# A planned scan-and-gate kernel: VectorE's steps in the head put into a fixed order, the fourth tile copied out by VectorE

## The chip, the cores and the metric

The kernel runs on one core of a Trainium2 chip. The metric is device time in microseconds (us). Before the change it is 181.62 us, the median of seven runs that lie between 181.51 and 181.90.

## The reference, cut to what matters

The input x is 2048 tokens by 512 channels. It is normalised per token, and two branches use the result. Branch A is a diagonal state space model: a complex projection, a recurrence over all 2048 tokens, a complex projection back and a skip. Branch B is a gated feed-forward net of width 1376. The output joins both.

```python
xn = layernorm(x)                       # per token, over 512 channels
Lam_bar = exp(dt * Lam)                 # dt = exp(log_dt), 512 complex numbers
Bu = einsum("bld,pd->blp", xn, ((Lam_bar - 1) / Lam)[:, None] * (B_re + 1j * B_im))
h[t] = Lam_bar * h[t-1] + Bu[t]         # t = 0 .. 2047
s = 2 * einsum("blp,dp->bld", h, C_re + 1j * C_im).real + xn * Dskip
g = silu((gelu(xn @ w_gate) * (xn @ w_up)) @ w_down)
out = x + s * g
```

All data are bf16.

## The kernel before, in words

**Tiling.** The tokens go in four stages of 512 (s = 0 to 3), each of four tiles of 128 tokens (m = 0 to 3). The matmuls need the normalised tile with the channels on the partitions, so each tile is turned. In stage 0, the head, TensorE turns it by four 128x128 transposes into half a PSUM bank (`transposed`, L415 to L425, called by `head_t`, L695), and ScalarE copies the result into `xnT` (L423). In the later stages a transposing DMA does it (`dma_t`).

**The head.** The first x tiles, the log step sizes, the gate weights `wg` and `wu` in three column chunks, the second stage's x, the projection BT and more weights are loaded one after the other; the SP queue issues them in a written chain (`dma_first`, L307, L331 to L343). For each tile, VectorE takes the statistics of 512 channels (L396), joins them (L399), adds a small constant to the variance (L405), POOL raises that to the power -0.5 (L402, tile `rs`), and VectorE normalises (L437, tile `xn`). In between VectorE also prepares the tables of cosines and sines: it copies the imaginary parts out of PSUM (L371), multiplies by the step size (L372), and does four steps on 196 angles (L656, L658, L659, L660), after which ScalarE takes two sines (L661, L662). POOL and ScalarE narrow these to bf16 (L664, L665), and VectorE builds the tables by six products and sums of 2048 columns (L676).

The first column chunk of gate and up matmuls of stage 0 (`gate_pair`, 384 columns, L470) runs tile by tile behind the transposes. It goes to three PSUM slots of two banks in turn; the fourth tile uses the two banks `ybank`, which the transposes use as well. The next chunk (512 columns) starts again with slot 0. ScalarE empties these banks by a copy (L475) and by the gelu (L476), which needs another function table than the sines; `early` orders the first gelu behind the sines. VectorE multiplies the two (L477).

`damping` (L687) turns four more small vectors by one tiny matmul (L690) through `ybank[0]`; its result, `rho`, is raised by POOL (L402) and needed by the scans.

**The body.** `half` (L592) projects with BT (L602), rotates by the tables (L616, L624 or L628), scans along time (L635) and rotates back. `gate_tile` and `down_pair` (L491, L534) are branch B; `y_tile` (L543) multiplies the states by C2 into `ybank` (L564), and VectorE joins the branches (L568 to L576). In the later stages ScalarE seeds `ybank` with the skip (L560). The output leaves by DMA on SP, one tile of 128 tokens at a time.

**What sets the order.** Each step is handed to a planner (`Plan`, L24) with its engine, an estimated cost, the time its result takes to reach others (`lag`), the names it reads and writes, and perhaps a rank. TensorE's steps are chained in the order in which the program adds them. The other engines' orders come from list scheduling by the longest remaining path plus rank, in six rounds forward and backward, and then from 3000 random trials on the start times, with a fixed seed, of which the best by the planner's own estimate is kept. The steps are then emitted by planned start. `after` adds an order without data; `_lag` (L59) says how long one step's end must lie before another's start. `urgent` (L391) gives the first two tiles' statistics and norms higher ranks.

Of the kernel before, what the change touches and what calls it, by code (L numbers as in the profile page):

```python
# [13 lines left out]
ALU = mybir.AluOpType  # L14
# [9 lines left out]
class Plan:  # L24

    def __init__(self):
        self.steps = []
        self.wrote = {}  # L30
        self.read = {}
        self.last_pe = None

    def add(self, eng, cost, emit, reads=(), writes=(), lag=0.05, table=None, not_before=0.0, rank=0.0, after=()):
# [161 lines left out]
def kernel(  # L196
# [17 lines left out]
    nc = tc.nc  # L214
    P = 128
# [174 lines left out]

    def urgent(s, m):  # L391
        return (60.0, 30.0, 0.0, 0.0)[m] if s == 0 else 0.0

    def stats(s, m):
        def f():
            V.bn_stats(out=st[:, s, m, :], in_=x_tok[:, s * M + m, :])  # L396
        rank = urgent(s, m)
        dve(512, f, [("x", s, m)], [("st", s, m)], base=0.12, rank=rank)
        dve(6, lambda: V.bn_aggr(out=mv[:, s, m, :], in_=st[:, s, m, :]), [("st", s, m)], [("mv", s, m)], base=0.08, rank=rank)  # L399

# [3 lines left out]
    def rstd(s, a, b):  # L404
        dve(b - a, lambda: V.tensor_scalar(out=ve[:, s, a:b], in0=mv[:, s, a:b, 1], scalar1=EPS, scalar2=None, op0=ALU.add),  # L405
            [("mv", s, m) for m in range(a, b)], [("ve", s, m) for m in range(a, b)], rank=urgent(s, a))
        power(rs[:, s, a:b], ve[:, s, a:b], mhalf[:, a:b], b - a, [("ve", s, m) for m in range(a, b)] + ["mhalf"], [("rs", s, m) for m in range(a, b)])
# [28 lines left out]
    def norm_dve(s, m):  # L436
        dve(512, lambda: V.tensor_scalar(  # L437
            out=xn[m][:], in0=x_tok[:, s * M + m, :], scalar1=mv[:, s, m, 0:1], scalar2=rs[:, s, m : m + 1],
            op0=ALU.subtract, op1=ALU.mult), [("x", s, m), ("mv", s, m), ("rs", s, m)], [("xn", m)], rate=2.0, rank=urgent(s, m))

    def dma_t(s, m):
        c0 = (s % 2) * TS + m * P
        return dma(SP, 1.2, 4.5 if s == 1 else 1.3, lambda: nc.sync.dma_start_transpose(out=xnT[:, :, c0 : c0 + P], in_=xn[m][:]),
            [("xn", m)], [("xnT", s % 2, m)])

# [7 lines left out]
    def gate_pair(s, m, c, then=((), ()), spare=False):  # L453
# [13 lines left out]
        for bank, (nm, wt) in enumerate((("wg", wg), ("wu", wu))):  # L467
            def f(bank=bank, wt=wt):
                for k in range(KT):
                    T.matmul(pss[bank][:, 0:w], lhsT=xnT[:, k, t0 : t0 + P], rhs=wt[:, k, a:b], start=(k == 0), stop=(k == KT - 1))  # L470
            pe(KT, w, f, [("xnT", s % 2, m), (nm, c)], [both[bank]])
            for t in then[bank]:
                t()
# [5 lines left out]
    def gate_tile(s, m):  # L479
# [14 lines left out]
        for kind, (nm, wt, dst) in enumerate((("wg", wg, gt[q]), ("wu", wu, ub[q]))):  # L494
            i, ps = slot()
            for c in range(2):
                pe(KT, 512, mm(ps, c, wt, c), [("xnT", s % 2, m)] + [(nm, n) for n in range(3)], [("slot", i, c)])
            fn = AF.Gelu_apprx_tanh if kind == 0 else AF.Copy
            acts(1024, lambda ps=ps, dst=dst, fn=fn: act(out=dst[:, 0:1024].rearrange("p (c w) -> p c w", c=2), in_=ps[:, :, :], func=fn),  # L499
                 [("slot", i, 0), ("slot", i, 1)], qs[kind], table="gelu" if kind == 0 else None)  # L500
        i, ps = slot()
        a, b = CH[2]
        for kind, (nm, wt) in enumerate((("wg", wg), ("wu", wu))):
            pe(KT, b - a, mm(ps, kind, wt, 2), [("xnT", s % 2, m)] + [(nm, n) for n in range(3)], [("slot", i, kind)])
        for kind, (nm, wt, dst) in enumerate((("wg", wg, gt[q]), ("wu", wu, ub[q]))):
# [86 lines left out]
    def half(s, h):  # L592
# [3 lines left out]
        for q in range(H2):  # L596
            i, ps = slot()
            pt = h * H2 + q
            for ri in range(2):
                def f(ri=ri, pt=pt, ps=ps):  # L600
                    for k in range(KT):
                        T.matmul(ps[:, ri, :], lhsT=BT[:, ri, k, pt * P : (pt + 1) * P], rhs=xnT[:, k, (s % 2) * TS : (s % 2 + 1) * TS],  # L602
                                 start=(k == 0), stop=(k == KT - 1))
                pe(KT, 512, f, [("BT", ri)] + [("xnT", s % 2, m) for m in range(M)], [("slot", i, ri)])
            acts(1024, lambda q=q, ps=ps: act(out=U[ui][:, :, q, :], in_=ps[:, :, :], func=AF.Copy),  # L605
# [44 lines left out]
        turn(Ff, hst[s % 2][:, :, hs, :].rearrange("p r q t -> p r (q t)"), allf, [("hst", s % 2, h)] + (CTS if s == 1 else []), False)  # L650

    def tables():
        NB4 = [P, NPT, NA, NB // 2, 2]
        sh, ch = sb("sh", [P, NPT, NB]), sb("ch", [P, NPT, NB])
        sp, cp = sb("sp", [P, NPT, NA, 2]), sb("cp", [P, NPT, NA, 2])
        dve(196, lambda: V.tensor_tensor(out=ang[:], in0=iota_f[:].unsqueeze(1).to_broadcast(W3), in1=thn.unsqueeze(2).to_broadcast(W3), op=ALU.mult),  # L656
            ["iota", "thn"], ["ang"])
        dve(196, lambda: V.tensor_scalar(out=kr[:], in0=ang[:], scalar1=MAGIC, scalar2=MAGIC, op0=ALU.add, op1=ALU.subtract), ["ang"], ["kr"], rate=2.0)  # L658
        dve(196, lambda: V.tensor_tensor(out=ang[:], in0=ang[:], in1=kr[:], op=ALU.subtract), ["kr"], ["ang", "kr"])  # L659
        dve(196, lambda: V.scalar_tensor_tensor(out=kr[:], in0=ang[:], scalar=-1.0, in1=ang[:], op0=ALU.mult, op1=ALU.max), ["ang"], ["kr"], base=0.13)  # L660
        early.append(acts(196, lambda: act(out=sbt[:], in_=ang[:], func=AF.Sin, scale=TWO_PI), ["ang"], ["sbt"], table="silu", rank=20.0))  # L661
# [110 lines left out]
    def norm1():  # L772
        for m in range(M):
            stats(1, m)
        rstd(1, 0, M)
        for m in range(M):
# [97 lines left out]
```

## Time and profile before

| what | value |
|---|---|
| median of seven runs | 181.62 us |
| the profiled execution | 181.54 us, span 179.8 us |
| TensorE busy | 173.8 us, 97% of the span |
| VectorE busy | 157.3 us, 88% |
| ScalarE busy | 117.8 us, 66% |
| POOL busy | 11.4 us, 6% |
| first gate matmul of the head | starts at 6.51 us |
| first matmul of the second column chunk | starts at 13.28 us |
| last matmuls | 175.19 us, for 1.04 us |
| granted TensorE clock | 1.0 in every stretch |

The span runs from the first to the last recorded instruction of the one core; the run's own time is 1.74 us more. A row of the timeline gives the start and the duration in us, engine, line, operation, the tile written and the tiles read, and how many instructions were merged; in brackets, how long the engine had been idle and what ended that. Matmuls are pipelined, and their ends are modelled, so the pace of TensorE is better read from the distance of two starts than from a duration. The chain follows the last instruction back, at each step to what released it. A row of the waits gives the engine and line, what it waited for, the time in total, the number of waits and the longest one.

### The profile page before, as it was taken

The numbers are of one execution on the slowest core, as the hardware profiler recorded it, in microseconds if no ns is written. First come the engines' busy times: TensorE is split into PE (matmuls) and PEld (weight loads), VectorE is DVE, ScalarE is ACT, GpSimd is POOL, SyncE is SP. The second block draws the span as 40 slices with busy tenths as digits, with TensorE's granted clock in tenths as the row PEclk, the third lists the DMA queues.
The fourth block names the chain that finished last, engine by engine and source line by source line (L and its number), as shares of the span: only waits on it lengthen the run. The fifth ranks groups of instructions, "written<-read, shape, count | busy, mean of one in ns | idle before, by whom it ended". The sixth has DMA issues, their size and how long they took to land.

```text
span 179.8 us, 2398 instructions
## 1 busy us (share of the span) xinstructions
PE 173.8 (97%) x838; PEld 83.0 (46%) x854; DVE 157.3 (88%) x267; ACT 117.8 (66%) x179; POOL 11.4 (6%) x19
## 2 busy tenths in 40 slices
PE   7999999999999999999999999999999999999992
PEld 2454444444445555444445554444445555444451
DVE  3889799999999999999999999999999999750063
ACT  4699599599998999747269953637418666443220
POOL 3450400000030000000020000000000000000000
PEclk9999999999999999999999999999999999999999
DMA  5999999997000449140022560451100071820011
GB/s 137 330 292 213 368 174 205 277 191 138 0 0 0 84 89 149 39 80 0 10 80 62 114 134 0 80 109 35 58 0 2 0 139 26 158 90 29 0 58 59
DMA packets 47109, 18.01 MB, mean 100 GB/s; under 512 B 38425, under 2 KB 47098, under 8 KB 47098
## 3 DMA queue, kind: packets, MB, share of 16 engines
q1 hardware_dynamic: 47072, 17.86, 45.3%
q8 instruction: 6, 0.10, 0.2%
q14 instruction: 5, 0.04, 0.1%
q10 hardware_dynamic: 26, 0.00, 0.0%
HBM read 6.33 MB, written 2.10 MB: 47 GB/s over the span
## 4 chain that ended last, share of the span: by engine, by line
PE 59%; DVE 31%; ACT 3%; issue 2%; POOL 1%; DMA 1%; DVEq 0%
PE slot L491 21%; PE slot L534 16%; PE ybank L564 11%; PE slot L602 8%; DVE Fs L635 7%; DVE Q L616 6%; PE slot L412 2%; DVE at L477 2%; DVE C L809 1%; DVE W L624 1%; DVE hst L624 1%; DVE Q L676 1%; DVE tab L676 1%; POOL rs L402 1%; DVE at L509 1%
## 5 line engine op out<-in xcount | busy, mean ns | idle before, releaser
L491 PEld LDWEIGHTS <-xnT 128*128 128x128 bf16 x288 | 28.2, 98 | 28.4
L534 PE MATMUL slot<-wd,atT 128*128 128x512 bf16 (+1 forms) x173 | 38.5, 379 | 0.2
L491 PE MATMUL slot<-wg,xnT 128*128 128x512 bf16 (+1 forms) x140 | 31.6, 356 | 0.3
L491 PE MATMUL slot<-wu,xnT 128*128 128x512 bf16 (+1 forms) x144 | 31.8, 357 | 0.0
L635 DVE TENSOR_TENSOR_SCAN Fs<-rho,ini,W 128x512 bf16<-128x512 f32 x24 | 29.3, 1266 | 0.0
L602 PE MATMUL slot<-xnT,BT 128*128 128x512 bf16 x124 | 28.1, 379 | 0.2
L564 PE MATMUL ybank<-C,hst 128*128 128x512 bf16 (+1 forms) x124 | 27.5, 372 | 0.3 <-ACT ybank L560 0.2
L534 PEld LDWEIGHTS <-atT 128*128 128x128 bf16 (+1 forms) x176 | 17.2, 98 | 20.9
L605 ACT ACTIVATE U<-slot 128x1024 bf16<-128x1024 f32 x16 | 16.1, 1019 | 9.7 <-PE slot L602 9.7
L568 DVE TENSOR_TENSOR yg<-ybank,g 128x512 bf16<-128x512 f32 (+1 forms) x14 | 9.4, 669 | 13.7 <-PE ybank L564 13.3
L564 PEld LDWEIGHTS <-hst 128*128 128x128 bf16 x136 | 13.3, 98 | 14.1 <-issue 0.4
L602 PEld LDWEIGHTS <-BT 128*128 128x128 bf16 x128 | 12.5, 98 | 15.1
L616 DVE TENSOR_TENSOR Q<-U,tab 128x4096 bf16<-128x4096 bf16 x8 | 18.3, 2287 | 0.3
L616 DVE TENSOR_TENSOR Q<-Fs,tab 128x4096 bf16<-128x4096 bf16 x8 | 18.3, 2285 | 0.1
L560 ACT ACTIVATE ybank<-sk 128x512 f32<-128x512 bf16 (+1 forms) x14 | 8.2, 586 | 15.2 <-DVE yg L568 14.5
L538 ACT ACTIVATE g<-slot 128x1024 f32<-128x1024 f32 x8 | 8.2, 1019 | 14.5 <-PE slot L534 14.5
L499 ACT ACTIVATE ub<-slot 128x1024 bf16<-128x1024 f32 x12 | 12.3, 1022 | 3.3 <-PE slot L491 3.2
L499 ACT ACTIVATE gt<-slot 128x1024 bf16<-128x1024 f32 x12 | 12.3, 1023 | 2.6 <-PE slot L491 2.5
L470 PEld LDWEIGHTS <-xnT 128*128 128x128 bf16 x96 | 9.1, 98 | 9.8 <-ACT xnT L423 0.7
L470 PE MATMUL slot<-wg,xnT 128*128 128x480 bf16 (+2 forms) x43 | 10.4, 360 | 0.4 <-ACT xnT L423 0.3
L786 ACT ACTIVATE junk<-x_tok 128x512 bf16<-128x512 bf16 x16 | 10.0, 627 | 1.1 <-DMA x_tok<-in_A_x_dram 0.9
L470 PE MATMUL slot<-wu,xnT 128*128 128x512 bf16 (+2 forms) x44 | 10.5, 360 | 0.0
(117 smaller groups left out, 180.9 us busy)
## 6 DMA issues: line engine op xcount, KB each, us to landing
out_dram<-ot SPq DMA_DIRECT2D x15, 128.0 KB, 1.7
x_tok<-in_A_x_dram SPq DMA_DIRECT2D x3, 512.0 KB, 6.1
wd<-in_B_w_down_dram SPq DMA_DIRECT2D x1, 1280.0 KB, 9.2
x_tok<-in_A_x_dram SPq DMA_DIRECT2D x4, 128.0 KB, 2.8
wg<-in_B_w_gate_dram SPq DMA_DIRECT2D x1, 512.0 KB
wu<-in_B_w_up_dram SPq DMA_DIRECT2D x1, 512.0 KB, 6.7
wg<-in_B_w_gate_dram SPq DMA_DIRECT2D x1, 480.0 KB, 4.9
wu<-in_B_w_up_dram SPq DMA_DIRECT2D x1, 480.0 KB
```

The costliest lines, as they stand in the source:

```text
L470: T.matmul(pss[bank][:, 0:w], lhsT=xnT[:, k, t0 : t0 + P], rhs=wt[:, k, a:b], start=(k == 0), stop=(k == KT - 1))
L491: T.matmul(ps[:, bank, 0 : b - a], lhsT=xnT[:, k, t0 : t0 + P], rhs=wt[:, k, a:b], start=(k == 0), stop=(k == KT - 1))
L499: acts(1024, lambda ps=ps, dst=dst, fn=fn: act(out=dst[:, 0:1024].rearrange("p (c w) -> p c w", c=2), in_=ps[:, :, :], func=fn), [("slot", ...
L534: T.matmul(ps[:, b, :], lhsT=atT[:fs, k, m * P : (m + 1) * P], rhs=wd[:fs, k, :], start=(k == 0), stop=(k == NFT - 1))
L538: acts(1024, lambda: act(out=g2[gi][:, :, :], in_=ps[:, :, :], func=AF.Silu), [("slot", i, 0), ("slot", i, 1)], [("g2", gi)], table="silu" ...
L564: T.matmul(bank, lhsT=hst[s % 2][:, j // NPT, j % NPT, m * P : (m + 1) * P], rhs=C2[:, j // NPT, j % NPT, a:z], start=(j == 0 and not seed ...
L568: dve(w, lambda: V.tensor_tensor(out=yg[e][:, a:z], in0=bank, in1=g2[gi][:, b, a:z], op=ALU.mult), [key, ("g2", gi)], [("yg", e, a)], base ...
L602: T.matmul(ps[:, ri, :], lhsT=BT[:, ri, k, pt * P : (pt + 1) * P], rhs=xnT[:, k, (s % 2) * TS : (s % 2 + 1) * TS], start=(k == 0), stop=(k ...
L605: acts(1024, lambda q=q, ps=ps: act(out=U[ui][:, :, q, :], in_=ps[:, :, :], func=AF.Copy), [("slot", i, 0), ("slot", i, 1)], [("U", ui, q)])
L616: dve(4096, lambda: V.tensor_tensor(out=Qf, in0=src.unsqueeze(1).to_broadcast(WQ), in1=table, op=ALU.mult), reads, ["Q"], rate=2.0)
L635: pl.add(DVE, 1.116 if s == 0 else 1.19, lambda ri=ri, q=q, pt=pt, first=first: V.tensor_tensor_scan(out=Fs[:, ri, q, :], data0=rho[:, pt ...
L786: acts(512, lambda i=i, fn=fn, m=m: act(out=junk[:], in_=x_tok[:, s * M + m, :], func=fn, accum_out=sx[:, s, i, m : m + 1]), [("x", s, m)] ...
```

## The change

VectorE's steps of the first four tiles' statistics and norms, the two small angle inputs and the four angle steps are put into one fixed order: while `pl.in_turn` is set, each VectorE step gets the one before as `after`. The angle inputs leave `columns` for `turn_angles`, and the angle steps leave `tables` for `angle(i)`; they stand between the second and fourth tile's steps. The second tile's norm now comes before the third tile's statistics. `bn_aggr` is a step of its own (`mean`), and the ranks of `urgent` are gone. The fourth tile's turned data are copied out of PSUM by VectorE, not by ScalarE, and its transposes stand behind the gate group of the third tile (TensorE's chain), not behind the up group of the second. Estimated landing times of five loads, and two cost estimates, are changed. `_lag` now gives a real lag to a step that is both ordered and read. `turned_tile` names what was named in place.

```diff
+        if eng == DVE and self.in_turn:
+            if self.last_dve is not None:
+                after = [*after, self.last_dve]
+            self.last_dve = n
...
-        if a in self.steps[b][8]:
+        if a in self.steps[b][8] and a not in self.steps[b][9]:
             return 0.0
...
-    load_x(SP, nc.sync, 2, 2.1)
-    load_first(0, 1, 2.2)
-    load_x(SP, nc.sync, 3, 2.2)
-    load_first(1, 0, 2.6)
-    load_first(1, 1, 2.8)
+    load_x(SP, nc.sync, 2, 2.55)
+    load_first(0, 1, 3.1)
+    load_x(SP, nc.sync, 3, 2.9)
+    load_first(1, 0, 3.5)
+    load_first(1, 1, 3.5)
...
+    def turn_angles():
         dve(4, lambda: V.tensor_copy(out=lim, in_=rows[:, NPT : 2 * NPT]), [("slot", 2, 0)], ["lim"], base=0.14)
         dve(4, lambda: V.tensor_tensor(out=thn, in0=lim, in1=dt_, op=ALU.mult), ["lim", "dt"], ["thn"])
...
-    def urgent(s, m):
-        return (60.0, 30.0, 0.0, 0.0)[m] if s == 0 else 0.0
...
+    def mean(s, m):
+        dve(6, lambda: V.bn_aggr(out=mv[:, s, m, :], in_=st[:, s, m, :]), [("st", s, m)], [("mv", s, m)], base=0.1)
...
+    def angle(i):
+
+        if i == 0:
+            dve(196, lambda: V.tensor_tensor(out=ang[:], in0=iota_f[:].unsqueeze(1).to_broadcast(W3), in1=thn.unsqueeze(2).to_broadcast(W3), op=ALU.mult),
+                ["iota", "thn"], ["ang"])
+        elif i == 1:
+            dve(196, lambda: V.tensor_scalar(out=kr[:], in0=ang[:], scalar1=MAGIC, scalar2=MAGIC, op0=ALU.add, op1=ALU.subtract), ["ang"], ["kr"])
+        elif i == 2:
+            dve(196, lambda: V.tensor_tensor(out=ang[:], in0=ang[:], in1=kr[:], op=ALU.subtract), ["kr"], ["ang", "kr"])
+        else:
+            dve(196, lambda: V.scalar_tensor_tensor(out=kr[:], in0=ang[:], scalar=-1.0, in1=ang[:], op0=ALU.mult, op1=ALU.max), ["ang"], ["kr"], base=0.13)
...
-        transposed(xn[m], m, xnT[:, :, m * P : (m + 1) * P], [("xn", m)], [("xnT", 0, m)], m % 2, ACT)
+        transposed(xn[m], m, xnT[:, :, m * P : (m + 1) * P], [("xn", m)], [("xnT", 0, m)], m % 2, DVE if m == 3 else ACT)
...
-    for m in range(M):
-        stats(0, m)
-        rstd(0, m, m + 1)
-        norm_dve(0, m)
+    pl.in_turn = True
+    stats(0, 0)
+    mean(0, 0)
+    rstd(0, 0, 1)
+    stats(0, 1)
+    mean(0, 1)
+    norm_dve(0, 0)
+    rstd(0, 1, 2)
     head_t(0)
     dummies(2, 0, 3)
+    turn_angles()
+    angle(0)
+    norm_dve(0, 1)
+    stats(0, 2)
+    mean(0, 2)
+    rstd(0, 2, 3)
+    angle(1)
+    stats(0, 3)
+    norm_dve(0, 2)
+    mean(0, 3)
+    rstd(0, 3, 4)
+    angle(2)
+    angle(3)
+    norm_dve(0, 3)
+    pl.in_turn = False
     tables()
-    then = {0: ((lambda: head_t(1), spread), ()), 1: ((lambda: head_t(2),), (lambda: head_t(3),))}
+    then = {0: ((lambda: head_t(1), spread), ()), 1: ((lambda: head_t(2),), ()), 2: ((lambda: head_t(3),), ())}
```

In `then`, the first entry of a pair is what TensorE does behind a tile's gate group, the second what it does behind its up group.

More of the change, by code (lines that the diff above doesn't have):

```diff
@@ L32, in __init__ @@
         self.last_pe = None
+        self.in_turn = False
+        self.last_dve = None
     def add(self, eng, cost, emit, reads=(), writes=(), lag=0.05, table=None, not_before=0.0, rank=0.0, after=()):
@@ L396, in f @@
             V.bn_stats(out=st[:, s, m, :], in_=x_tok[:, s * M + m, :])
-        rank = urgent(s, m)
-        dve(512, f, [("x", s, m)], [("st", s, m)], base=0.12, rank=rank)
-        dve(6, lambda: V.bn_aggr(out=mv[:, s, m, :], in_=st[:, s, m, :]), [("st", s, m)], [("mv", s, m)], base=0.08, rank=rank)
+        dve(512, f, [("x", s, m)], [("st", s, m)], base=0.12)
+    def mean(s, m):
+        dve(6, lambda: V.bn_aggr(out=mv[:, s, m, :], in_=st[:, s, m, :]), [("st", s, m)], [("mv", s, m)], base=0.1)
     def power(out, base, exponent, n, reads, writes):
@@ L405, in rstd @@
         dve(b - a, lambda: V.tensor_scalar(out=ve[:, s, a:b], in0=mv[:, s, a:b, 1], scalar1=EPS, scalar2=None, op0=ALU.add),
-            [("mv", s, m) for m in range(a, b)], [("ve", s, m) for m in range(a, b)], rank=urgent(s, a))
+            [("mv", s, m) for m in range(a, b)], [("ve", s, m) for m in range(a, b)])
         power(rs[:, s, a:b], ve[:, s, a:b], mhalf[:, a:b], b - a, [("ve", s, m) for m in range(a, b)] + ["mhalf"], [("rs", s, m) for m in range(a, b)])
@@ L438, in norm_dve, with turned_tile @@
             out=xn[m][:], in0=x_tok[:, s * M + m, :], scalar1=mv[:, s, m, 0:1], scalar2=rs[:, s, m : m + 1],
-            op0=ALU.subtract, op1=ALU.mult), [("x", s, m), ("mv", s, m), ("rs", s, m)], [("xn", m)], rate=2.0, rank=urgent(s, m))
+            op0=ALU.subtract, op1=ALU.mult), [("x", s, m), ("mv", s, m), ("rs", s, m)], [("xn", m)], rate=2.0)
+    def turned_tile(s, m):
+        return [("xnT", s % 2, m)]
     def dma_t(s, m):
@@ L443, in dma_t @@
         return dma(SP, 1.2, 4.5 if s == 1 else 1.3, lambda: nc.sync.dma_start_transpose(out=xnT[:, :, c0 : c0 + P], in_=xn[m][:]),
-            [("xn", m)], [("xnT", s % 2, m)])
+            [("xn", m)], turned_tile(s, m))
     def skip(s, m):
@@ L470, in f @@
                     T.matmul(pss[bank][:, 0:w], lhsT=xnT[:, k, t0 : t0 + P], rhs=wt[:, k, a:b], start=(k == 0), stop=(k == KT - 1))
-            pe(KT, w, f, [("xnT", s % 2, m), (nm, c)], [both[bank]])
+            pe(KT, w, f, turned_tile(s, m) + [(nm, c)], [both[bank]])
             for t in then[bank]:
@@ L496, in gate_tile @@
             for c in range(2):
-                pe(KT, 512, mm(ps, c, wt, c), [("xnT", s % 2, m)] + [(nm, n) for n in range(3)], [("slot", i, c)])
+                pe(KT, 512, mm(ps, c, wt, c), turned_tile(s, m) + [(nm, n) for n in range(3)], [("slot", i, c)])
             fn = AF.Gelu_apprx_tanh if kind == 0 else AF.Copy
@@ L503, in gate_tile @@
         for kind, (nm, wt) in enumerate((("wg", wg), ("wu", wu))):
-            pe(KT, b - a, mm(ps, kind, wt, 2), [("xnT", s % 2, m)] + [(nm, n) for n in range(3)], [("slot", i, kind)])
+            pe(KT, b - a, mm(ps, kind, wt, 2), turned_tile(s, m) + [(nm, n) for n in range(3)], [("slot", i, kind)])
         for kind, (nm, wt, dst) in enumerate((("wg", wg, gt[q]), ("wu", wu, ub[q]))):
@@ L603, in f @@
                                  start=(k == 0), stop=(k == KT - 1))
-                pe(KT, 512, f, [("BT", ri)] + [("xnT", s % 2, m) for m in range(M)], [("slot", i, ri)])
+                pe(KT, 512, f, [("BT", ri)] + [k for m in range(M) for k in turned_tile(s, m)], [("slot", i, ri)])
             acts(1024, lambda q=q, ps=ps: act(out=U[ui][:, :, q, :], in_=ps[:, :, :], func=AF.Copy),
@@ L655, in tables @@
         sp, cp = sb("sp", [P, NPT, NA, 2]), sb("cp", [P, NPT, NA, 2])
[L656 to L660, printed above, removed]
         early.append(acts(196, lambda: act(out=sbt[:], in_=ang[:], func=AF.Sin, scale=TWO_PI), ["ang"], ["sbt"], table="silu", rank=20.0))
@@ L774, in norm1 @@
             stats(1, m)
+            mean(1, m)
         rstd(1, 0, M)
```

## The prediction

> **What bounds the kernel now.** I read the busy table first, then the waits, the chain, and the rows of the first 21 us.
>
> ```profile
> PE 173.8 (97%) x838; PEld 83.0 (46%) x854; DVE 157.3 (88%) x267; ACT 117.8 (66%) x179; POOL 11.4 (6%) x19
> ...
> PE ybank L564 <- ACT ybank L560: 0.2, 1, 0.2
> ```
>
> TensorE works nearly all the time; the only wait on another engine after the head is 0.2 us. A check by pitch: sixteen 512-column matmuls take 3.46 us (103.23 to 106.69), four 480-column ones 0.81, four 352-column ones 0.59 to 0.60. From the second group of gate matmuls, at 13.28, to the last y group, at 169.14, lie 624, 32 and 96 of them: 134.9 + 6.5 + 14.3 = 155.7 us, against 155.86 that passed. So some 0.2 us can be won between 13.28 and 169.14. The rest must come from the head or the tail.
>
> The chain, read through the head:
>
> ```profile
> 6.46 0.05 issue
> 6.51 0.82 PE slot L470 x4
> 7.33 0.22 PE ybank L420 x4
> ...
> 9.54 0.60 ACT xnT L423
> 10.14 0.25 ACT sbt L661
> 10.39 0.35 ACT cbt L662
> 10.74 0.49 ACT xnT L423
> 11.22 0.20 ACT sp L665
> 11.42 0.02 issue
> 11.44 1.28 ACT L476
> ...
> 14.98 0.63 DVE at L477 x2
> ```
>
> Here ScalarE carries the end: two sines, the copy-out of the fourth tile, a narrowing copy, the load of the gelu table. From 14.98 the chain stays on VectorE, with one POOL step of 2.26 us, until 73.40, and then on TensorE. So two engines are nearly level: a TensorE gain stands only if VectorE is no later at 73.40.
>
> TensorE in the head, by starts:
>
> ```profile
> 7.17 0.39 PE L420 MATMUL ybank<-ident,xn 128*128 128x128 bf16 x4
> 9.12 0.39 PE L420 MATMUL ybank<-ident,xn 128*128 128x128 bf16 x4
> 9.99 0.39 PE L420 MATMUL ybank<-ident,xn 128*128 128x128 bf16 x4
> 12.38 0.81 PE L470 MATMUL ybank<-wu,xnT 128*128 128x384 bf16 x4
> 12.74 0.49 ACT L476 ACTIVATE gt<-slot 128x384 bf16<-128x384 f32 x1
> 13.28 1.02 PE L470 MATMUL slot<-wg,xnT 128*128 128x512 bf16 x3
> ```
>
> A group of four 384-column matmuls passes in 0.65 us (11.08 to 11.73), so the group at 12.38 is through at 13.03. The next reuses slot 0, which the gelu frees at 12.74 + 0.49 = 13.23: 0.25 us idle. From 6.51 to 13.28 are 6.77 us; the work is 8 x 0.65 + 3 transposes x 0.22 + 0.22 for the skip-row matmul + about 0.06 = 6.14. The other 0.4 are pauses of about 0.1 around the two tiny matmuls, which stay.
>
> **The change, part by part.** VectorE up to the second variance step (5.08) keeps its order, so the first tile and the matmul at 6.51 stay. From there, with pitches of these rows (statistics to aggregate 0.73, aggregate to variance 0.22, dependent small step 0.18, variance to POOL's result about 0.8, POOL's result to norm 0.08):
>
> - angle inputs 5.15 and 5.33, first angle step 5.52;
> - second norm when rs is there (5.30 + 0.56, then 0.08): 5.94 to 6.33, before 7.01;
> - third statistics 6.26, aggregate 6.99, variance 7.21, its rs about 8.05; second angle step 7.28; fourth statistics 7.55;
> - third norm 8.18 to 8.58, before 8.08; fourth variance 8.69, its rs about 9.5;
> - third and fourth angle steps 8.77 and 9.16, through at 9.13 and 9.52, before 9.31 and 9.92;
> - fourth norm 9.61 to 10.01, before 9.64.
>
> What of this lies on the path? The second norm, 0.7 us earlier, is worth nothing: its transpose ran at 7.17, when the gate group begun at 6.51 was through (7.16), and TensorE's order is kept. The third norm loses 0.5 us, but its transpose comes at 9.12: 0.5 us of cover. The angle steps come 0.2 and 0.4 us earlier. VectorE is through with the list at 9.93 against 9.83 (the next step began there): 0.1 us later. The 0.38 us hole at 5.22, a wait for the third x tile, is filled, but two short waits for POOL (about 0.15 each) come instead.
>
> **The fourth tile** has two edits. TensorE transposes it after the third tile's first group, not before it. Now the eviction of the third tile (9.54 to 10.14) stands bare: the group at 9.34 is through at 9.99, and both the tiny matmul, which reuses the same bank, and the next group wait until 10.19, 0.20 us. Before, the transpose (0.22) filled this. After that: tiny matmul 10.19, group 10.30, transpose 10.95 to 11.17, group 11.17 to 11.82, its records ending at 11.34. VectorE's copy has no row. It lies between 0.40 (the norm, 128x512 bf16 in SBUF) and 0.68 (128x512 f32 out of PSUM). I take 0.41: a four-element copy from PSUM lasts 0.16, only 0.01 to 0.03 over such steps in SBUF, and the norm's slope is (0.40 - 0.15)/512 per element; the data are bf16. Then the copy runs 11.37 to 11.78, the fourth tile's first group starts at 11.83, its second at 12.48, and slot 0's next at 13.13. With 0.68 it is 13.40.
>
> The Trainium skill (VectorE: DVE Perf Modes, section Why PSUM operands drop a tier) says a PSUM operand allows at most the packed double rate, and only for 16-bit data; an estimate by its table of cycles is 0.39 us, which would give 13.12. No row of this profile shows it.
>
> **ScalarE** loses one 0.58 us copy-out, and the sine steps' inputs come earlier. In the old order the next step follows the second sine at 10.64; with the narrowing copy (0.32 to the next start) still ahead, the table load goes to 10.96 from 11.44, the gelu ends near 12.75 instead of 13.23, and slot 0 is free before TensorE comes. So 13.13 to 13.15 instead of 13.28: **-0.15 us**.
>
> **VectorE afterwards.** It gets 0.41 for the copy and 0.10 from above. Its holes at 12.75 (0.51) and 14.80 (0.17), both waits for the gelu, close if ScalarE is half a us earlier: 0.68 - 0.51 = 0.17 us ahead, about what removes the 0.15 us wait at 74.07. I count **-0.10 us**, since this is a difference of larger terms; bounds +0.5 (neither hole closes) and -0.2 (no more than TensorE's idle time).
>
> The Trainium skill (Perfetto Trace Analysis, section Optimizing Scalar/DVE Operations) speaks against this part: where VectorE is saturated, work should go to ScalarE. The row agrees that it is (19.90 of 20.00 us busy between 40 and 60). By the rule alone the sum would be +0.41 - 0.15 against the profiled time; the holes above are why I don't take it.
>
> **Nothing by themselves:** the chain over VectorE's steps, the removed ranks, and the new landing and cost figures only feed the planner; the landing chain on SP keeps its order, so no load moves. No moved step issues a DMA. POOL gets the same four square roots; its two narrowing copies and the 2.01 us damping power (11.62) follow, and a power put ahead of a narrowing copy would hold the table products. BT, the gate weights and the next x tiles are issued as before; if one landed only in time for TensorE at 20.18, the 0.15 would be lost again.
>
> But the planner searches at random from other figures, so every later order on VectorE, ScalarE and SP can come out differently. Nothing in the profile prices this below -0.2 (idle time left); upwards a wait like the 0.91 us at 19.2 (VectorE for POOL's rs) is the nearest row.
>
> **Sum:** 181.54 (the profiled execution: 179.8 span + 1.74 around it) - 0.15 - 0.10 = 181.29, say **181.3**. The median, 181.62, lies 0.08 above that execution; 0.2% of it, 0.36 us, is about what a measurement of this kernel tells from no change. So the forecast lies at the edge: 181.26 would be faster.
>
> **Rivals.**
> 1. *The copy comes late (slower).* VectorE's order is written out by the plan; if it puts a table product (1.22 us, 1.15 to the next start) ahead of the copy, which the earlier narrowed sines allow, the copy starts up to 1.15 after 11.37. It decides once the copy starts later than about 11.5: from there TensorE loses all of it. Half of a product costs 0.58 - 0.15, a whole one 1.0: 182.0 to 182.5. For it: the product began at 11.53 before. Against: the copy's high rank in the plan.
> 2. *VectorE's path gets longer.* The holes do not close (+0.5) and the new plan has one more wait like the 0.91 one. TensorE then waits near 74: +0.5 - 0.15 to +1.4 - 0.15, 181.9 to 182.8. For it: almost no slack from 14.98 to 73.40. Against: the 0.91 wait could go as well.
> 3. *All that is idle goes.* The new plan also hides the third eviction and the wait at 74: -0.25 - 0.2 and a little: 180.9 to 181.1.
> 4. *Nothing moves:* ScalarE's plan keeps the table load at 11.44: 181.5 to 181.6.
>
> **How the numbers follow.** Forecast 0.38 (own range 181.05 to 181.55), rival 1 0.20, rival 2 0.16, rival 3 0.20, rival 4 0.06. Faster by 0.2%: 0.20 of rival 3 and 0.17 of the forecast's range, 0.37. Slower: rivals 1 and 2, 0.36. Within: 0.27. The range leaves out less than 0.1 on each side: 180.8 to 182.6.
>
> **What would show it.** Right: second norm near 5.9, transposes still at 7.17 and 9.12, a group near 10.2 that waited for ScalarE, a copy of about 0.41 on VectorE at 11.4, table load before 11.2, slot 0's next group near 13.13 with no wait, no wait at 74. Wrong: the copy waiting behind a table product, a wait of TensorE between 20 and 80, or another tail after the last matmul.

## The result, and the profile after

The changed kernel takes 181.12 us (median of 27 runs, 180.77 to 181.90); the kernel before takes 181.70 (median of 69, 181.39 to 182.90). The ratio is 0.9966, with a 95% interval of 0.9958 to 0.9974: 0.34% faster. The profiled execution of the changed kernel took 180.90 us, its span 179.1, at a mean granted clock of 0.997. Profile against profile the gain is 0.64 us.

The busy table of the changed kernel, and the shares of its chain by engine:

```profile
PE 172.8 (96%) x838; PEld 82.6 (46%) x854; DVE 158.0 (88%) x268; ACT 117.1 (65%) x178; POOL 9.8 (5%) x19
...
PE 94%; DVE 1%; ACT 1%; DMA 1%; issue 1%; DVEq 0%
```

VectorE is busier by 0.7 us, and still it has left the chain. Three pieces of that chain (start, length, engine, tile, line) show it: they are TensorE where the old chain had ScalarE's table load and then VectorE up to 73.40.

```profile
11.13 0.65 PE slot L480 x4
11.78 1.34 PE ybank L480 x8
...
70.15 5.18 PE ybank L574 x24
```

The timeline of the changed kernel in the head. Lines have moved: L430 and L432 are the copies out of PSUM by ScalarE and VectorE, L444 the norm, L480 the gate and up groups, L486 the gelu and its table, L707 the tiny matmul.

```profile
5.91 0.41 DVE L444 TENSOR_SCALAR xn<-x_tok,mv,rs 128x512 bf16<-128x512 bf16 x1
...
6.31 0.82 PE L480 MATMUL slot<-wg,xnT 128*128 128x384 bf16 x4 [0.36 <-ACT xnT L430]
...
8.92 0.39 PE L427 MATMUL ybank<-ident,xn 128*128 128x128 bf16 x4
9.14 0.81 PE L480 MATMUL slot<-wu,xnT 128*128 128x384 bf16 x4
9.34 0.60 ACT L430 ACTIVATE xnT<-ybank 128x512 bf16<-128x512 bf16 x1 [0.38 <-PE ybank L427]
...
9.99 0.16 PE L707 MATMUL ybank<-ident,pv 4*128 4x4 bf16 x1
...
10.56 1.28 ACT L486 ACT_TABLE_LOAD   x1
...
11.16 0.42 DVE L432 COPY xnT<-ybank 128x512 bf16<-128x512 bf16 x1 [0.48 <-PE ybank L427]
...
11.85 0.49 ACT L486 ACTIVATE gt<-slot 128x384 bf16<-128x384 f32 x1
...
12.96 1.03 PE L480 MATMUL slot<-wg,xnT 128*128 128x512 bf16 x3
```

The reader is to see three things. The group at 9.14 is through at 9.79 (9.14 + 0.65), and the tiny matmul starts at 9.99: 0.20 us bare behind the third tile's eviction. The copy on VectorE waits for TensorE, not the other way. And the gelu ends at 12.34, long before slot 0 is wanted at 12.96, so the old wait there is gone.

The y group before the third stage's projection, first in the kernel before, then in the changed one:

```profile
70.30 3.62 PE L564 MATMUL ybank<-C,hst 128*128 128x512 bf16 x16
74.07 1.89 PE L564 MATMUL ybank<-C,hst 128*128 128x512 bf16 x8 [0.15 <-ACT ybank L560]
75.79 6.42 PE L602 MATMUL slot<-xnT,BT 128*128 128x512 bf16 x28
```

```profile
69.98 5.34 PE L574 MATMUL ybank<-C,hst 128*128 128x512 bf16 x24
75.16 7.07 PE L612 MATMUL slot<-xnT,BT 128*128 128x512 bf16 x31
```

From start to start the 24 matmuls took 5.49 us before and 5.18 after. So 0.31 us went, although the wait's bracket said 0.15.

Where the 0.64 us between the two profiles went, by starts on TensorE:

| stretch | before | after | difference |
|---|---|---|---|
| to the first gate matmul | 6.51 | 6.31 | -0.20 |
| from there to the second column chunk | 6.77 | 6.65 | -0.12 |
| from there to the y group at 70 | 57.02 | 57.02 | 0.00 |
| y group at 70 to the projection | 5.49 | 5.18 | -0.31 |
| from that projection to the last matmuls | 99.40 | 99.40 | 0.00 |

The first row isn't the change's doing in these two executions: the transposes of the first tile start at 5.22 in both. Before, they still ran at the long pitch (four in 0.61 us, after 0.40), so the first eviction began at 5.86 instead of 5.66. When the pitch shortens differs from one execution to the next: the same head starts its first gate matmul at 6.23 to 6.43 in the runs below.

### The profile page after: what moved, and what is told of

Same layout as the page of the kernel before. It is cut to its first block, busy times and chain, and to the rows that moved or that the text cites. A ratio compares the mean times of both kernels' runs of the same rounds, so it can differ in the third digit from the quotient of the medians.

```text
span 179.1 us, 2392 instructions
## 1 busy us (share of the span) xinstructions
PE 172.8 (96%) x838; PEld 82.6 (46%) x854; DVE 158.0 (88%) x268; ACT 117.1 (65%) x178; POOL 9.8 (5%) x19
## 3 DMA queue, kind: packets, MB, share of 16 engines
HBM read 6.33 MB, written 2.10 MB: 47 GB/s over the span
## 4 chain that ended last, share of the span: by engine, by line
PE 94%; DVE 1%; ACT 1%; DMA 1%; issue 1%; DVEq 0%
PE slot L501 31%; PE slot L544 21%; PE slot L612 15%; PE ybank L574 13%; PE slot L480 10%; PE slot L419 2%; DMA out_dram<-ot 1%; DVE ot L586 1%; PE ybank L480 1%; ACT L377 1%; DVE yg L578 1%; PE ybank L427 0%; ACT xnT L430 0%; PE slot L716 0%; ACT tiny L377 0%
## 5 line engine op out<-in xcount | busy, mean ns | idle before, releaser
L480 PEld LDWEIGHTS <-xnT 128*128 128x128 bf16 x96 | 9.0, 98 | 9.7 <-ACT xnT L430 0.7
L480 PE MATMUL slot<-wg,xnT 128*128 128x480 bf16 (+2 forms) x43 | 10.4, 360 | 0.4 <-ACT xnT L430 0.4
L480 PE MATMUL slot<-wu,xnT 128*128 128x512 bf16 (+2 forms) x44 | 10.5, 360 | 0.0
```

## The experiments

Where a run below re-creates one half of the change, the planner's freedom had to be taken out. `BODY` holds the planned starts of another kernel's steps off TensorE; the list scheduling then follows them:

```diff
-        start = best[1]
+        key = [BODY.get(self.names[i], best[1][i]) for i in range(n)]
+        start, length = self._decode(pairs, key)
```

In what follows, "gate to projection" is the distance from the first gate matmul to the first projection with BT (13.67 us before, 13.55 after), and "y to projection" the distance of the two rows above (5.49 and 5.18). A median is given with its ratio to the kernel before on the same chip; the medians of the kernel before there were 181.74 to 181.76.

### Both kernels once more

Edit: none; first the changed kernel.

> The changed kernel once more, beside the kernel before on the same chip, to see what repeats. In the two profiles the first gate matmul starts at 6.31 us (after) and 6.51 (before), because the filler matmuls reach the short pitch (0.216 us instead of 0.43) at about 4.2 us in one and only after 5.6 in the other. If that belongs to the change, this profile shows 6.31 again; if it is chance, it may show either, and the gain of the change is 0.2 us smaller than the two profiles say. Time either way near 181.1 us, ratio 0.996 to 0.998. The start of the second column chunk should lie 6.65 us behind the first gate matmul (6.77 before).

Measured: 181.08 us, ratio 0.9958 (0.9944 to 0.9972). Gate to projection is 13.55 again, y to projection 5.24; the first gate matmul starts at 6.25. The profiled execution itself took 181.35, because one wait came that the first profile doesn't have, here in the timeline of this run:

```profile
33.19 5.34 PE L612 MATMUL slot<-xnT,BT 128*128 128x512 bf16 x23
38.81 1.89 PE L612 MATMUL slot<-xnT,BT 128*128 128x512 bf16 x8 [0.28 <-ACT U L615]
40.54 1.67 PE L544 MATMUL slot<-wd,atT 128*128 128x512 bf16 x7
```

The stretch took 7.35 us (33.19 to 40.54) against 6.91 in the first profile (33.25 to 40.16): 0.44 lost, of which the bracket shows 0.28. So the changed kernel has waits that come and go as well.

Then the kernel before.

> The kernel before once more, one profile. If the wait near 74 us belongs to it, the distance from the first y group after 69 us to the next projection group is 5.49 us again (5.18 is the work alone). The first gate matmul may start anywhere from 6.2 to 6.5 if the start of the short pitch is chance, and at 6.5 if it is the kernel's.

Measured: 182.04 us, one execution. The wait at 74 is there again (y to projection 5.50), and the first gate matmul starts at 6.42, so its place is chance in both kernels. The run shows one thing that spreads the times of the old kernel. Timeline of this run:

```profile
6.18 0.69 DVE L396 BATCH_NORM_STATS2 st<-x_tok 128x6 f32<-128x512 bf16 x1 [1.12 <-DMA x_tok<-in_A_x_dram]
...
7.20 0.40 DVE L437 TENSOR_SCALAR xn<-x_tok,mv,rs 128x512 bf16<-128x512 bf16 x1
...
7.66 0.40 PE L420 MATMUL ybank<-ident,xn 128*128 128x128 bf16 x4 [0.42 <-DVE xn L437]
```

VectorE stood 1.12 us at the third tile's statistics, because its x tile landed late. The second tile's norm stands behind them in the old order, and TensorE waited for that norm. Gate to projection became 14.26, 0.59 more than in the first profile. In the first profile the same wait was 0.38 and hidden.

### Which half of the plan brings it

First the changed kernel's head with the old order: `BODY` holds the planned starts of the kernel before from 20 us on.

```diff
+BODY = {
...
+}
```

> The changed kernel, but all steps that both plans put at 20 us or later are emitted in the order of the kernel before (VectorE, ScalarE, POOL and SP; TensorE's order is the same anyway). Theory A, the wait near 74 us went because VectorE left the head earlier: no wait there, 181.1 us, the same as the changed kernel. Theory B, it went because the search found another order for the body: the wait of about 0.3 us is back, the head's 0.12 us stays, 181.4 to 181.5 us, ratio 0.998 to 0.9995.

Measured: 181.03 us, ratio 0.9955 (0.9942 to 0.9969); gate to projection 13.55, y to projection 5.18. The new head alone gives all that the change gives, the wait at 74 included; the first gate matmul starts at 6.42 here.

VectorE's rows between the head and the body say how. First the kernel before, then this run (L769, L801 and L1050 are its L405, L437 and L676):

```profile
17.57 0.16 DVE L405 TENSOR_SCALAR ve<-mv 128x4 f32<-128x4 f32 x1
...
20.11 1.38 DVE L437 TENSOR_SCALAR xn<-x_tok,mv,rs 128x512 bf16<-128x512 bf16 x4 [0.91 <-POOL rs L402]
...
21.74 1.22 DVE L676 TENSOR_TENSOR tab<-Q 128x2048 bf16<-128x2048 bf16 x1
```

```profile
17.54 0.17 DVE L769 TENSOR_SCALAR ve<-mv 128x4 f32<-128x4 f32 x1
...
19.09 1.05 DVE L801 TENSOR_SCALAR xn<-x_tok,mv,rs 128x512 bf16<-128x512 bf16 x3
...
21.05 1.22 DVE L1050 TENSOR_TENSOR tab<-Q 128x2048 bf16<-128x2048 bf16 x1
```

At the second stage's four variances VectorE isn't ahead yet (17.57 and 17.54). POOL then raises the four in one step: 2.25 us in the kernel before, 1.12 here. The wait of 0.91 behind that step is gone, and VectorE stands 0.69 ahead at the table sum and still 0.54 at the product that empties `ybank` (L572, 72.72 before, 72.18 here). ScalarE has seeded `ybank` again at 73.48, only 0.07 before TensorE wants it (70.09 + 3.46 = 73.55). In the old head POOL does the long damping power first (11.62); here that comes at 26.29. Why the step takes half as long is not shown.

Now the other way round, in the kernel before: `BODY` holds the planned starts of the changed kernel from 20 us on.

```diff
+BODY = {
...
+}
```

> The kernel before, but all steps that both plans put at 20 us or later are emitted in the order of the changed kernel. Theory A: the head is the old one, so the slot wait at 13.28 and the wait near 74 both stay: 181.6 us, ratio 0.9995 to 1.001. Theory B: the slot wait stays, the wait near 74 is gone: 0.3 us less, 181.3 us, ratio 0.998.

Measured: 181.44 us, ratio 0.9985 (0.9974 to 0.9997); gate to projection 13.73, y to projection 5.19. So the other order of the body also removes the wait at 74, without any gain in the head: POOL's step takes 2.25 us and VectorE waits 0.91 for it as before, but the product that empties `ybank` now stands 1.93 us behind the start of the y group (70.34 to 72.27) instead of 2.42. The wait stands in the three profiles of old head with old body (5.49, 5.50, and 5.49 in the run with the second norm put first, below), and in neither mixture. Either half is enough, and the two gains don't add.

### How much is the planner's luck

```diff
-        rng = random.Random(1)
+        rng = random.Random(2)
```

> The changed kernel with another seed of the planner's random search (2 for 1), nothing else. If what the search happens to find weighs as much as the change, the time moves by 0.2 to 0.6 us either way (180.9 to 181.7) and the waits of TensorE between 20 and 80 us come or go; if the head alone makes the gain, it stays within 0.1 us of the changed kernel, 181.0 to 181.2.

Measured: 181.27 us, ratio 0.9971 (0.9955 to 0.9986), and the same 13.55 and 5.18. The gain doesn't hang on the one seed; 0.1 to 0.2 us, within the intervals, is all that another plan changed.

### The order without the copy, and the copy without the order

The order alone: the fourth tile is copied out by ScalarE, at its old place on TensorE.

```diff
-... m % 2, DVE if m == 3 else ACT)
+... m % 2, ACT)
...
-    then = {..., 1: ((lambda: head_t(2),), ()), 2: ((lambda: head_t(3),), ())}
+    then = {..., 1: ((lambda: head_t(2),), (lambda: head_t(3),))}
```

> The changed kernel without its fourth-tile edits: ScalarE copies that tile out, and its transposes stand behind the second tile's up group again; from 20 us on the order is the changed kernel's. If the 0.12 us between the first gate matmul and the second column chunk comes from the tile's copy leaving ScalarE, that distance is 6.75 to 6.85 us here, with the slot wait back; if it comes from the fixed order, it is 6.65. The wait near 74 should stay away, since the body's order is the new one. Time about 181.4 us in the first case, 181.1 to 181.2 in the second.

Measured: 181.43 us, ratio 0.9986 (0.9977 to 0.9995). Gate to projection is 14.00, worse than the 13.67 of before; y to projection is 5.18, the body being the changed kernel's. Timeline of this run:

```profile
9.63 0.41 DVE L806 TENSOR_SCALAR xn<-x_tok,mv,rs 128x512 bf16<-128x512 bf16 x1
...
10.10 0.40 PE L789 MATMUL ybank<-ident,xn 128*128 128x128 bf16 x4
...
12.50 0.81 PE L842 MATMUL ybank<-wu,xnT 128*128 128x384 bf16 x4
13.49 1.02 PE L842 MATMUL slot<-wg,xnT 128*128 128x512 bf16 x4 [0.18 <-ACT gt L848]
```

The new order ends with the fourth norm at 10.04, and the transposes at the old place follow it, at 10.10. ScalarE copies that out at 11.06 and loads the gelu table at 11.66; slot 0 is late by 0.34 (12.50 + 0.65 to 13.49). From the first gate matmul to the second column chunk are 7.10 us, more than either case had (6.65 to 6.85). By itself the order has nothing to give here.

The copy alone: before's order of VectorE, with the fourth tile's two edits.

```diff
-... m % 2, ACT)
+... m % 2, DVE if m == 3 else ACT)
...
-    then = {..., 1: ((lambda: head_t(2),), (lambda: head_t(3),))}
+    then = {..., 1: ((lambda: head_t(2),), ()), 2: ((lambda: head_t(3),), ())}
```

> The kernel before with the fourth tile's two edits alone (VectorE copies it, transposes behind the third tile's gate group), the old rules for VectorE's order in the head, and the changed kernel's order from 20 us on. If the tile's edits make the head's gain, the distance from the first gate matmul to the second column chunk is 6.65 us, as in the changed kernel, and the time 181.1 to 181.2 us; if the fixed order makes it, the distance stays near 6.77 and the time near 181.4.

Measured: 181.72 us, ratio 0.9999 (0.9990 to 1.0008); gate to projection 13.99, y to projection 5.18. The third tile's statistics waited for their load until 5.70, the second transposes came 0.24 late, the third eviction stood bare, and the table load, at 11.54, gained nothing: this plan put both narrowing copies and a copy-out of up data ahead of it. The gelu ended at 13.33, and slot 0 waited for it. The distance to the second column chunk is 7.09 us, again more than either case had. As the planner arranges them, neither half improves the head; together they give -0.12. Another plan for a half alone was not tried.

### The second norm ahead of the third statistics

That edit alone, in the kernel before, all other orders held:

```diff
+        n = norm_dve(0, m)
+        held[0, m + 1] = [n] if m == 1 else ()
...
-        dve(512, f, [("x", s, m)], [("st", s, m)], base=0.12, rank=rank)
+        dve(512, f, [("x", s, m)], [("st", s, m)], base=0.12, rank=rank, after=held.get((s, m), ()))
```

> The kernel before with one edit: VectorE's norm of the second tile stands ahead of the third tile's statistics; every other step of every engine keeps the order of the kernel before. Theory C: the gain that the profiles do not show comes from the third x tile landing late in many executions (VectorE waited for it until 5.60, 5.61, 5.70 and 6.18 us in the four looks at this order), which holds up the second norm behind it, the transpose behind that and so TensorE: 0.1 to 0.4 us gained here, 181.35 to 181.65, and the transpose starts 0.66 us behind the first gate matmul whenever the tile lands. The prediction's reading, that the second norm is worth nothing: no change, 181.75.

Measured: 182.20 us, ratio 1.0020 (1.0004 to 1.0037): slower. Timeline of this run, in which L841 is the copy of the imaginary parts out of PSUM and L1171 the skip row's matmul:

```profile
5.79 0.41 DVE L909 TENSOR_SCALAR xn<-x_tok,mv,rs 128x512 bf16<-128x512 bf16 x1 [0.68 <-POOL rs L874]
...
7.42 0.38 PE L1171 MATMUL slot<-Drow,junk 1*128 1x512 bf16 x1
...
7.92 0.16 DVE L841 COPY pf<-slot 128x4 f32<-128x4 f32 x1 [0.71 <-PE slot L1171]
...
10.62 0.40 PE L892 MATMUL ybank<-ident,xn 128*128 128x128 bf16 x4 [0.52 <-DVE xn L909]
```

The second transposes were on time (7.10). But the norm now waited 0.68 for POOL with nothing to fill it. Then the copy, at its old place ahead of the fourth statistics, waited 0.71: the profile puts that down to the skip row's matmul, which uses the same slot. The fourth statistics and norm slid behind it, and the fourth transposes came 0.68 late by starts (9.29 + 0.65 to 10.62; the bracket says 0.52). Gate to projection: 14.35. Both readings missed the time; since other waits took over, the run doesn't tell what the place of the norm by itself is worth.

And the reverse, the second norm put back behind the third tile's variance, in the changed kernel:

```diff
-    norm_dve(0, 1)
     stats(0, 2)
     mean(0, 2)
     rstd(0, 2, 3)
+    norm_dve(0, 1)
```

> The changed kernel with one edit: VectorE's norm of the second tile stands behind the third tile's statistics, aggregate and variance, as before; every other step keeps the changed kernel's order. Theory C: the norm ends at the statistics' start plus 1.4 us, 7.2 to 7.6 us, the transpose that wants to start at 6.9 to 7.05 starts 0.3 to 0.6 us late, and the time is 181.4 to 181.7. The prediction's reading: no change, 181.1.

Measured: 181.27 us, ratio 0.9971 (0.9960 to 0.9981). The norm starts at 6.77, the second transposes at 7.23, 0.12 after the gate group is through, and gate to projection is 13.67. So the place of this norm is worth 0.12 in this profile. The third statistics, at 5.76, waited for no load here. The median (181.27 against 181.12) points the same way, but the intervals overlap, and it lies below the 181.4 to 181.7 of theory C.

### What room VectorE has left

After the copy of the fourth tile, two more copies of it, into a tile that nobody reads:

```diff
+        if m == 3:
+            for _ in range(2):
+                dve(512, lambda: V.tensor_copy(out=spare[:], in_=ybank[1][:].bitcast(BF16)[:, 0:D]), [("y", 1), ("xnT", 0, 3)], ["spare"], rate=2.0, rank=40.0)
```

> The changed kernel with two more copies of the fourth tile by VectorE (into a spare tile, right behind the first), that is 0.7 to 0.85 us more of VectorE's time at 11.6 us; every other step keeps its order. If VectorE is level with TensorE from 15 to 74 us, as the chain of the kernel before has it, what exceeds its slack comes out as a wait of TensorE before 76 us: 181.4 to 181.8. If VectorE has half a us or more of slack in the new order, 181.1 to 181.3.

Measured: 181.76 us, ratio 1.0002 (0.9991 to 1.0012). Timeline of this run:

```profile
12.63 0.42 DVE L1186 COPY spare<-ybank 128x512 bf16<-128x512 bf16 x1
13.10 0.81 PE L950 MATMUL ybank<-wu,xnT 128*128 128x384 bf16 x4 [0.50 <-DVE spare L1186]
```

The price was paid at once and by TensorE, since the copies hold the bank that the fourth tile's up group writes: 0.68 us (11.77 + 0.65 to 13.10). Gate to projection went to 14.22, 0.67 more. y to projection stayed at 5.18. By starts the two copies cost VectorE 0.34 and 0.33 us (11.96 to 12.30, 12.63 to 12.96), not the 0.42 of their rows, so VectorE had 0.67 more to do and TensorE came 0.67 later. What room VectorE has at 74 this run can't tell, because the bank came first.

### Can it be bettered?

Three tiles copied out by VectorE instead of one:

```diff
-... m % 2, DVE if m == 3 else ACT)
+... m % 2, ACT if m == 1 else DVE)
...
+    turn_angles()
     head_t(0)
     dummies(2, 0, 3)
-    turn_angles()
...
```

> The changed kernel with the first and third tile copied out by VectorE too (the angle steps one place later), orders searched anew. The copy lasts 0.42 us on VectorE against 0.60 on ScalarE in the profiles. If the copy-outs bound the head, the first gate matmul starts 0.18 us earlier behind its transposes and the 0.2 us that TensorE waits for the third tile's copy shrinks to nothing: 180.7 us. If VectorE has no more room, its 0.84 us come back as a wait of TensorE near 74 us: 181.0 to 181.5.

Measured: 181.21 us, ratio 0.9970 (0.9960 to 0.9980); gate to projection 14.02 in a profile whose TensorE ran at the long pitch in the first gate group (1.04 us instead of 0.66). The first gate matmul came 1.13 us behind its transposes (5.12 to 6.25), against 1.29 in the run before this one, which had the long pitch there too, and the third eviction stood bare for 0.10 instead of 0.20. But VectorE's fourth norm, at 10.67, was late, and the fourth transposes waited 0.18 for it (10.31 + 0.65 to 11.14). No better.

The first and third tile copied half by ScalarE, half by VectorE, from two banks:

```diff
+        acts(256, lambda: act(out=dst[:, 0:2, :], in_=tps[0], func=AF.Copy), [("y", 0)], writes[:1], rank=100.0)
+        dve(256, lambda: V.tensor_copy(out=dst[:, 2:4, :], in_=tps[1]), [("y", 1)], writes[1:], rate=2.0, rank=40.0)
```

> The changed kernel, with the first and the third tile's transposes laid into two banks, of which ScalarE copies one half out and VectorE the other; orders searched anew. Both copies stand bare on TensorE's path (0.6 us ahead of the first gate matmul, 0.2 us behind the second tile's up group). If nothing else takes over, the first gate matmul starts 0.2 us earlier behind its transposes and the second wait is gone: 180.7 us, faster than both. If VectorE's or POOL's chain to the second norm takes over, the transposes of the second tile wait instead: 181.0 to 181.2.

Measured: 181.38 us, ratio 0.9989 (0.9965 to 1.0013). The first gate matmul came at 6.09, the earliest of all, 0.87 behind its transposes; gate to projection is 13.68, and the profiled execution took 180.85. But the twelve runs spread from 180.81 to 182.94. Why they spread wasn't found. It isn't a better kernel as it stands.

## Why the prediction was right, and where it was off

The forecast was 181.3 us within 180.8 to 182.6, with faster as the likeliest sign by a hair. The time is in the range and the sign is right, but the gain is more than twice as large: 0.58 between the medians and 0.64 between the profiles, against a sum of 0.25. Part of the 0.64 is chance (0.20, the pitch), and half of it (0.31) came by a way that the sum didn't have.

**The head: right.** "-0.15" was said from the first gate matmul on; -0.12 was measured. The steps behind it held: second norm 5.91 to 6.32 (said 5.94 to 6.33), third norm 8.01 (8.18), fourth 9.61 (9.61), the bare third eviction 0.20 (0.20), no wait at slot 0, and the fourth transposes 0.66 after the group before them (0.65). All of TensorE's starts lie 0.20 earlier than said, by the chance of the pitch.

**The copy: right.** 0.42 us against 0.41, near the lower bound, as the 16-bit data suggested. The prediction's estimate by the cycle table of the Trainium skill (VectorE: DVE Perf Modes, section The TRN2 errata) was 0.39; the trace shows 0.42, 0.03 us above it. That agrees with the double rate which the page allows a PSUM operand (section Why PSUM operands drop a tier).

**ScalarE: right in kind, too cautious.** The table load was put at 10.96 with the narrowing copy ahead of it; it came at 10.56, because the plan puts both narrowing copies behind the first gelu (12.24 and 14.66), and because all starts lie 0.20 earlier. The gelu ended at 12.34 instead of 12.75. TensorE had no use for the difference.

**The wait at 74: mis-sized, and gone by another way.** I counted "-0.10" out of "the 0.15 us wait at 74.07". It was 0.31. The bracket measures to the end of a matmul's record, and these ends are modelled: sixteen matmuls have a record of 3.62 us here, and the prediction's own check had them at 3.46. Had I subtracted starts, as in the head, the wait would have been 74.07 - 70.30 - 3.46 = 0.31, and the sum 181.54 - 0.15 - 0.31 = 181.08 at full removal. The bound of -0.2 below fell with it. It rested on a count of 155.7 us of matmuls against 155.86 passed, and at 624 matmuls a pitch off by 0.0003 us is 0.2 us: 24 of them in 5.18 give 0.2158, where 16 in 3.46 had given 0.2163. A bound made of the difference of two such sums can't be trusted to 0.2.

VectorE's lead was mis-sized as well. The prediction had VectorE 0.17 us ahead, from two holes behind the gelu less the copy and the longer list. That was too little for the wait even as sized there, since TensorE itself comes earlier: 0.31 + 0.12 = 0.43 was needed. The two holes did close (the product with the first gelu comes at 12.38 with no idle time before it), but a new hole of 0.48 ahead of the copy and 0.35 for the copy itself (11.16 to 11.51) use that up, and at 17.5 VectorE was not ahead. The lead came from the third hole, the 0.91 behind POOL's step, which the prediction named, as a risk and as something that "could go as well", and left out of its sum. The old order of the body with the new head has the wait gone and that hole gone; all four profiles with POOL's 2.25 us have the hole. No run changed POOL's step alone. So the right sign of this term was partly luck.

**The second norm "is worth nothing": wrong outside the one profile.** By the profile of before the transposes had 0.15 us to spare (norm through at 7.01, gate group at 7.16). Four profiled executions with VectorE's old order show its third statistics beginning at 5.60, 5.61, 5.70 and 6.18, always behind the load, and the second transposes late for that norm by 0.24 and 0.59 in the last two, and on time in the first two. In the third of them the load came only 0.10 later than in the first; there TensorE was ready 0.22 earlier (first gate matmul at 6.29), by the chance of the pitch. So the cover shrinks from both sides. With the changed order the third statistics begin at 6.09 to 6.23, behind the norm, and waited for no load in any profile. The fourth statistics did wait for theirs (0.21 and 0.54 in two profiles), and it was hidden: gate to projection was 13.55 in all four profiles of the whole change. I priced the mean of a wait by one sample, and named its cover without asking how the landing varies.

**What stays open.** The head and the wait at 74 explain 0.43 of the 0.58 between the medians. Late landings in the old order would account for the rest, and 12 of the 69 runs of the kernel before lie above 182.0 against none of the 27 after. But the lowest times also differ by 0.62 (181.39 and 180.77), how often the load lands late was not measured, and the two runs meant to test it missed its forecast (182.20 against 181.35 to 181.65, where other waits took over, and 181.27 against 181.4 to 181.7). So this remainder is only argued.

**The rivals.** The late copy (1) didn't occur: the copy waited 0.48 for TensorE. VectorE's longer path (2) didn't either: its two holes closed, and the 0.91 wait went instead of doubling. The fourth, nothing moves, is ruled out by the table load. The third came closest: the time lies at its upper end, 0.02 above, and one of its two parts happened (the wait at 74), the other not (the third eviction is still bare).

**The rule against it.** The prediction set the Trainium skill's advice (Perfetto Trace Analysis, section Optimizing Scalar/DVE Operations) against the holes in VectorE's head. The page says only that giving some work of a saturated VectorE to ScalarE "may make sense". The measurement decides for the holes, the one behind POOL above all: VectorE does 0.7 us more and is off the chain. A share of busy time over the whole kernel said nothing on the 10 us in question.

## What to carry to other kernels

Size a wait on TensorE by the distance of two starts less the pitch of the work between, never by the idle time in a row: here every such row was 0.16 to 0.18 us short. An order on an in-order engine is priced by what is queued behind its latest input, over several executions if that input comes by DMA; the hidden 0.38 us wait of one profile was a 0.59 us loss in another. Test halves: the order and the copy each did nothing or harm for the head, and only together freed it. And when a wait goes, look which hole ahead of it closed: here it was not the one that the sum had counted on.

## What the runs showed of the hardware

- **Idle brackets against starts.** Four waits of TensorE, by bracket and by starts: 0.15 and 0.31 (the y group of before), 0.28 and 0.44 (the projection in the repeat of the changed kernel), 0.50 and 0.68 (the bank held by the extra copies), 0.52 and 0.68 (the fourth transposes in the run with the second norm first). A group of four 384-column matmuls has a record of 0.81 us and a pace of 0.65: the difference is the missing 0.16. The Trainium skill (Perfetto Trace Analysis, section Tensor Engine Instruction) states that TensorE's ends in the profile are estimated; these rows show by how much.
- **The start of the short pitch.** The three filler matmuls at 3.85 took 0.92 us in the profile after and 1.46 in most others, and in the run with three copies the first gate group, at 6.25, still took 1.04 to the next start instead of 0.66. The fillers begin at 1.05 or 1.06 in both of the main profiles. So the pitch shortened before 4.8 us in the one and not before 6.25 us in the other, while the granted clock in the profile's rows reads 1.00 throughout. The Trainium skill (TensorE: Matmul & The Clock Gate, section Part 1) gives the change of pace as varying by 0.5 us either way, and warns that the number of slow matmuls differs from run to run; here the spread was at least 1.45 us (from before 4.8 to after 6.25).
- **Copies out of PSUM.** 128x512 of bf16: 0.42 us on VectorE, 0.58 to 0.60 on ScalarE. By starts the next step follows sooner: 0.35 on VectorE (11.16 to 11.51 in the changed kernel), 0.48 on ScalarE (10.64 to 11.12 in the kernel before).
- **POOL's power of four columns.** The same step on 128x4 took 2.25 us in the four profiles in which the damping power ran some 6 us ahead of it, and 1.12 to 1.15 in nine of the ten others; in the run with the halved copies it took 1.92. VectorE's next norm began when it ended (20.07 and 20.11 in the kernel before). The cause is not shown.
